# Shifted copies of VectorE's exponentials, divided between VectorE and GpSimd in pieces of 512 columns, with a fifth copy buffer in memory that is dead at the time

## The chip, the cores and the metric

The kernel runs on one core of a Trainium2 chip. The metric is the device time of one execution in microseconds (us). Three runs of the kernel before took 821.25, 820.0 and 817.97 us; their median, 820.0 us, is what the change is held against. Engines are named as in the profile: PE (TensorE, matmuls), ACT (ScalarE), DVE (VectorE), POOL (GpSimd), SP (SyncE, which here only issues DMAs).

## What is computed

One transformer block with modulated layer norms: attention with 32 heads of 16 columns over 2048 tokens of width 512, then a gated feed-forward part with 1792 hidden columns. All tensors are bf16.

```python
def _A_ref(x, wqkv, wo):
    ...
    q, k, v = (qkv[0], qkv[1], qkv[2])
    scores = jnp.einsum('bhqd,bhkd->bhqk', q, k) * Dh ** (-0.5)
    p = _softmax(scores, axis=-1)
    o = jnp.einsum('bhqk,bhkd->bhqd', p, v)
    return (lambda x, *d: x.transpose(*d))(o, 0, 2, 1, 3).reshape(B, S, D) @ wo

def _B_ref(x, w_gate, w_up, w_down):
    return _gelu(x @ w_gate) * (x @ w_up) @ w_down
x = A_x
mod = (_silu(c) @ w_mod).reshape(c.shape[0], 6, 1, -1)
...
h = _layernorm(x, axis=-1) * (1 + ca) + sa
x = x + ga * _A_ref(h, A_wqkv, A_wo)
h = _layernorm(x, axis=-1) * (1 + cb) + sb
x = x + gb * _B_ref(h, B_w_gate, B_w_up, B_w_down)
```

The exponentials of the softmax are the bulk of the elementwise work: 32 x 2048 x 2048 of them, which the kernel handles as 2048 blocks of 128 keys by 512 query columns (or the same amount in narrower pieces).

## The kernel before

**Units, rounds, blocks.** Attention is cut into units (a set of queries, and a quarter of the heads of one parity, `qd` 0 to 7). `SETS` (L32) has nine query sets, seven of 256 queries and two of 128; the first two sets are also handled together at 512 columns for `qd` 0 to 3. A unit runs through the 16 key blocks in rounds; a round is four blocks of 512 columns, one for each of four heads. A round of a 256-column unit covers two key blocks, so such a unit has 8 rounds.

**A tick.** PE writes two or three blocks of scores into one half of six PSUM banks (`ps_sc`). ACT takes them in one instruction, `self.act(self.E..., ACT.Exp)` (L1620), into the ring `E`. The other half of the banks is filled meanwhile.

**VectorE's exponentials.** In many ticks one of the three blocks is not given to ACT. DVE turns it into an approximate exponential by writing `score * 128/OCT + SHIFT_C` as a 16-bit integer (L1628) that is then read as bf16: the integer's upper bits are the exponent, and the lower ones stand in for the mantissa. To make this more exact the kernel takes four versions: the integers as they are, and with 32, 64 and 96 added (`SHIFT`, L72). The added amounts are undone in copies of V (`vs`) that are scaled by the inverse power of two, and PE sums all four. A round handled in this way is called a quad here: four blocks are written to one of the buffers `kq` (four 128x512 instructions out of PSUM), and then three shifted copies of the whole 128x2048 buffer are made into buffers `sq` (three instructions within SBUF). `shift_task` (L1719) queues these copies, one task each. PE then has four sums over V for the round in place of one.

**Which rounds may become quads.** Only those of the last key blocks: `vs` holds copies for the key blocks from `T0` = 12 on (L45, L489). So a 256-column unit can give 2 of its 8 rounds; the first units can give more (`FIRST`, L57; `cand`, L1445). A candidate is dropped when its unit comes near its end (L1581). A quad is begun (L1589) when a `kq` buffer is free, no copy is overdue, DVE's list is short enough (`backlog`, L1283) and the side work isn't too far behind (`credit`).

**Who sets the order.** The kernel is written out by a planner at build time. `_Recorder.rec` (L183) takes each instruction, finds what it must wait for, and keeps a model of when each engine is free (`cost`, L301; `model`, L261). `stream` (L1380) asks this model at each step what could start now: the next tick, the sums over V (`pv_next`), side work (projections, output projection, feed-forward) or a task. `background` (L1291) and `step` (L1255) hand waiting tasks to SP and DVE, by `urgency` (L1243), whenever the model has the engine free. Each engine then executes its own list in that order, and waits for semaphores where it must. So the planner's times decide the order, and the chip's own times decide what that order costs.

**Buffers.** `sq` has four copy buffers (`NSQ`, L48), three of them in `mreg` and one of its own, and two more that serve in parts of the run: `ereg` (also the place of two pieces of the down weights) and half of `onorm`. `room` (L1449) says which may be used when. From when the modulation columns are there (`modB`), a unit has four; the first four units have `ereg` as a fifth.

**Weights.** For the first six sets the feed-forward weights are streamed anew for each set (`load` and `load_down`, L1128 to L1139); from set 6 on they are resident (`weight_parts`, L927), in tensors that attention has finished with. Piece 6 of the gate weights and of the down weights lie in `hreg`, behind `prodL`.

GpSimd does a few memsets and masks at the start, and nothing later.

## Time and profile before

| what | us |
|---|---|
| runs of the kernel before: lowest, median, highest | 817.97, 820.0, 821.25 |
| span of the profiled execution | 817.5 |
| ACT busy | 783.2 |
| PE busy | 750.5 |
| DVE busy | 742.8 |
| POOL busy | 4.6 |

The span runs from the first to the last instruction of the profiled execution; what lies around it (2.5 us to the median) isn't broken down by the profile, and the profiled execution's own time is given by its span alone. In a group of instructions, "mean ns of one" is the time from an instruction's start to its end. On DVE and ACT the next instruction starts before that end, so what an instruction costs its engine is read from the distance of two starts in the timeline, which is shorter. A timeline row gives start, length, engine, line, operation and operands; a row of groups gives count, busy time and mean, then the idle time in front and who ended it.

### The profile page before, as it was taken

The page shows a single profiled execution, that of the slowest core. Times are in us where ns is not written, and L with a number is a line of the kernel's source. Part 1 is how long each engine was busy: PE and PEld are TensorE (multiplying, and loading weights), DVE is VectorE, ACT ScalarE, POOL GpSimd, SP SyncE. Part 2 cuts the span into 40 slices and gives each one's busy share as a digit, 9 for nine tenths or more (in the row PEclk, how much of TensorE's full clock was granted, in tenths as well). Part 3 has the DMA queues.
Part 4 walks back from the last instruction along what each step waited for, and adds up shares of the span by engine and source line. Part 5 has one row for each costly group of instructions (what it writes and reads, how often), then busy time and mean ns, then how long its engine had stood idle before and what let it go on. Part 6 is the DMA issues. An engine that isn't in the chain of part 4 may idle for free.

```text
span 817.5 us, 37365 instructions
## 1 busy us (share of the span) xinstructions
PE 750.5 (92%) x17184; PEld 366.4 (45%) x17188; DVE 742.8 (91%) x1496; ACT 783.2 (96%) x746; POOL 4.6 (1%) x13
## 2 busy tenths in 40 slices
PE   7899999998999898989999899998998899888998
PEld 3333334343543454435443444444443444346567
DVE  6876898899999999999999999999999999989874
ACT  5999999999999999999999999999999999999962
POOL 2000000000000000000000000000000000000000
PEclk9999999999999999999999999999999999999999
DMA  9100000021530153104420442034233541200000
GB/s 292 63 6 20 10 9 10 10 71 40 168 112 16 52 155 93 35 21 134 122 63 16 136 121 61 16 105 133 63 106 88 165 126 36 67 10 10 19 13 14
DMA packets 94499, 57.38 MB, mean 70 GB/s; under 512 B 17029, under 2 KB 91910, under 8 KB 94342
## 3 DMA queue, kind: packets, MB, share of 16 engines
q1 hardware_dynamic: 93812, 54.47, 23.6%
q8 instruction: 134, 2.20, 1.2%
q10 hardware_dynamic: 530, 0.53, 0.2%
q14 instruction: 23, 0.19, 0.1%
HBM read 50.04 MB, written 2.35 MB: 64 GB/s over the span
## 4 chain that ended last, share of the span: by engine, by line
ACT 88%; PE 9%; DVE 1%; issue 0%; DMA 0%; SPq 0%; DVEq 0%
ACT E L341 85%; PE ps_sc L328 4%; PE ps_mi L328 3%; ACT wreg L341 3%; PE ps_pv L328 2%; DMA xs<-in_A_x_dram 0%; DVE osb L362 0%; DVE xs L345 0%; DVE dreg L353 0%; DVE st L381 0%; DVE wreg L353 0%; DVE nwt L345 0%; PE ps_sc L332 0%; DVE wreg L358 0%; DVE mreg L353 0%
## 5 line engine op out<-in xcount | busy, mean ns | idle before, releaser
L341 ACT ACTIVATE E<-ps_sc 128x1024 bf16<-128x1024 f32 (+2 forms) x700 | 758.7, 1319 | 19.1 <-PE ps_sc L328 19.0
L328 PE MATMUL ps_sc<-qT,kT 32*128 32x256 bf16 (+3 forms) x2048 | 202.2, 273 | 25.2 <-ACT E L341 21.1
L328 PE MATMUL ps_sc<-qo,kT 32*128 32x256 bf16 (+2 forms) x2048 | 202.2, 273 | 16.9 <-ACT E L341 15.5
L328 PE MATMUL ps_pv<-E,vaug 128*17 128x256 bf16 (+2 forms) x3204 | 154.1, 273 | 3.8 <-DVE osb L362 2.7
L353 DVE TENSOR_SCALAR dreg<-ps_sc 128x512 uint16<-128x512 f32 x200 | 135.5, 687 | 6.8 <-PE ps_sc L328 5.8
L328 PE MATMUL ps_mi<-wreg,mreg 128*32 128x256 bf16 x2816 | 116.6, 275 | 6.5 <-DVE wreg L362 3.4
L328 PEld LDWEIGHTS ps_sc<-qT,kT 32*128 32x128 bf16 (+1 forms) x2048 | 62.3, 92 | 117.3 <-ACT E L341 105.1
L328 PEld LDWEIGHTS ps_sc<-qo,kT 32*128 32x128 bf16 x2048 | 62.1, 92 | 105.6 <-ACT E L341 94.9
L328 PEld LDWEIGHTS ps_pv<-E,vaug 128*17 128x17 bf16 x3204 | 60.4, 89 | 59.6 <-issue 39.8
L328 PEld LDWEIGHTS ps_mi<-wreg,mreg 128*32 128x32 bf16 x2816 | 63.7, 96 | 42.8 <-issue 24.8
L328 PE MATMUL ps_pv<-mreg,vs 128*17 128x256 bf16 (+2 forms) x1840 | 80.9, 268 | 0.6 <-DVE mreg L353 0.3
L353 DVE TENSOR_SCALAR kq<-ps_sc 128x512 uint16<-128x512 f32 x104 | 70.9, 688 | 8.6 <-PE ps_sc L328 8.2
L353 DVE TENSOR_SCALAR mreg<-dreg 128x2048 uint16<-128x2048 uint16 x100 | 67.5, 682 | 2.2 <-PE ps_pv L328 2.2
L353 DVE TENSOR_SCALAR mreg<-ps_sc 128x512 uint16<-128x512 f32 x96 | 65.0, 688 | 4.5 <-PE ps_sc L328 4.3
L328 PEld LDWEIGHTS ps_pv<-mreg,vs 128*17 128x17 bf16 x1840 | 40.7, 91 | 15.1 <-issue 4.7
L353 DVE TENSOR_SCALAR mreg<-mreg 128x2048 uint16<-128x2048 uint16 x71 | 47.4, 686 | 0.0
L328 PE MATMUL ps_mi<-hreg,wreg 128*32 128x512 bf16 (+1 forms) x496 | 36.6, 376 | 0.4 <-DVE vaug L362 0.3
L362 DVE CAST wreg<-ps_mi 128x512 bf16<-128x512 f32 x49 | 33.6, 686 | 2.4 <-PE ps_mi L328 2.2
L345 DVE TENSOR_TENSOR wreg<-wreg 128x1024 bf16<-128x1024 bf16 (+1 forms) x56 | 34.5, 618 | 0.0
L353 DVE TENSOR_SCALAR sq<-dreg 128x2048 uint16<-128x2048 uint16 x49 | 33.7, 687 | 0.8 <-PE ps_pv L328 0.8
L358 DVE SCALAR_TENSOR_TENSOR wreg<-wreg,ps_mi 128x512 bf16<-128x512 bf16 x49 | 33.4, 682 | 1.0 <-ACT wreg L341 0.5
L353 DVE TENSOR_SCALAR mreg<-kq 128x2048 uint16<-128x2048 uint16 x48 | 32.5, 683 | 0.0
(193 smaller groups left out, 722.7 us busy)
## 6 DMA issues: line engine op xcount, KB each, us to landing
mreg<-in_B_w_up_dram SPq DMA_DIRECT2D x46, 256.0 KB, 3.2
mreg<-in_B_w_gate_dram SPq DMA_DIRECT2D x42, 256.0 KB, 3.3
dreg<-in_B_w_down_dram SPq DMA_DIRECT2D x18, 256.0 KB, 3.5
rb<-scr_rec SPq DMA_DIRECT2D x120, 32.0 KB, 2.0
mreg<-in_B_w_down_dram SPq DMA_DIRECT2D x12, 256.0 KB, 3.7
ereg<-in_B_w_down_dram SPq DMA_DIRECT2D x12, 256.0 KB, 3.8
mreg<-in_w_mod_dram SPq DMA_DIRECT2D x1, 2048.0 KB, 11.8
out_dram<-xs SPq DMA_DIRECT2D x15, 128.0 KB, 1.7
```

What stands on the lines that cost most here:

```text
L328: return self.rec("pe", lambda e: e.matmul(out, lhsT, rhs, start=start, stop=stop, tile_position=tp), [lhsT, rhs], [out], cost=(n, int(rhs ...
L341: return self.rec("act", lambda e: e.activation(out, in_, func, scale=scale, **kw), rd, wr, cost=self.cost("act", out, [in_], "act"))
L345: return self.rec(eng, lambda e: e.tensor_tensor(out, a, b, op), [a, b], [out], cost=self.cost(eng, out, [a, b], "tt"))
L353: return self.rec(eng, lambda e: e.tensor_scalar(out, a, s1, s2, **kw), rd, [out], cost=self.cost(eng, out, [a], "ts") + 60 * (len(rd) - 1 ...
L358: return self.rec("dve", lambda e: e.scalar_tensor_tensor(out, a, s, b, op0=op0, op1=op1), rd, [out], cost=self.cost("dve", out, [a, b], " ...
L362: return self.rec(eng, lambda e: e.tensor_copy(out, in_), [in_], [out], cost=self.cost(eng, out, [in_], "ts"))
```

## The change

Lines of the diff that only pass arguments on are left out.

```diff
+POOL = (0.834, 162)
+PIECE = 512
...
+    def shared(self, eng, out, ins):
+
+        sb = [a for a in ins if self.kind.get(a.tensor.name) == "sb"]
+        return eng == "pool" or len(sb) > 1 or (len(sb) == len(ins) == 1 and self.kind.get(out.tensor.name) == "sb")
...
-        at = 0.0
+        at = self.port_free if port and (eng == "pool" or self.probing is None) else 0.0
...
         self.model(op, max(at, self.free[eng]), cost)
+        if port:
+            self.port_free = op.t1 - 92
...
         if eng == "pool":
-            return n * 3.0 + 100
+            return n * POOL[0] + POOL[1]
...
-        self.sq += [ereg[:, :], onorm[:, 2048:4096]]
+        self.sq += [ereg[:, :], onorm[:, 2048:4096], hreg[:, NFC * 256:NFC * 256 + 2048], mreg[:, 10240:12288]]
...
-        return ([piece(0, i, g[i]) for i in range(6)] + [piece(0, 6, g[6], [("ffn", 0)]), piece(2, 6, d[6], [("ffn", 0)])]
+        return ([piece(0, i, g[i]) for i in range(6)] + [piece(0, 6, g[6], [last, "sq"]), piece(2, 6, d[6], [last, "sq"])]
...
-                self.task([("sp", lambda: self.dma("sp", self.wdst[i], v[:, 2 * i:2 * i + 2, :], "sd%d" % i))], ("wl", gi, 2, i))
+                self.task([("sp", lambda: self.dma("sp", self.wdst[i], v[:, 2 * i:2 * i + 2, :], "sd%d" % i))], ("wl", gi, 2, i),
+                          (lambda: NSQ in self.sq_free) if i > 4 else None)
...
-            e, f = tk[0][0]
+            e, f = tk[0][0][:2]
+            if e == "any":
+                if eng == "pool":
+                    e, f = tk[0][0][2][0]
+                else:
+                    e = "dve"
...
             f()
-            tk[0].pop(0)
+            x = tk[0].pop(0)
+            if x[0] == "any" and eng == "pool":
+                tk[0][0:0] = x[2][1:]
...
         while self.free["dve"] <= t + 150 and self.step("dve", max(self.free["dve"], t) + 40):
             pass
+        while self.free["pool"] <= t + 150 and self.step("pool", max(self.free["pool"], t) + 40):
+            pass
+        while self.free["act"] <= t - 300 and self.step("act", t):
+            pass
...
+            elif pool is self.quad_free:
+                ok = range(NK)
             else:
-                ok = range(NK if pool is self.quad_free else NSQ + (u in units[:4]))
+                ok = list(range(NSQ))
+                if ("ffn", FLOW - 1) in self.have:
+                    ok += [NSQ, NSQ + 3]
+                elif ("q", 3, NDC - 1) in self.have:
+                    ok += [NSQ + 2]
+                elif ("t2T", 0) not in self.have:
+                    ok += [NSQ]
...
+            if ("ffn", FLOW - 1) in self.have and NSQ + 2 in self.sq_free:
+                self.done("sq")
...
-                    elif (... and (pos < ends[FLOW - 1] or self.credit < self.tune[1] or ...
+                    elif (... and (pos < ends[0] or self.credit < self.tune[1] or ...
...
-        def f():
+        def whole():
             s = self.room(self.sq_free, q["rnd"][0])[0]
             self.ts("dve", self.sq[s].bitcast(U16), self.kq[q["k"]].bitcast(U16), float(SHIFT[i]), None, ALU.add)
...
+        def piece(a):
+            s = q["slots"][i + 1] if a else self.room(self.sq_free, q["rnd"][0])[0]
+            c = slice(a, a + PIECE)
+            self.ts("pool", self.sq[s][:, c].bitcast(U16), self.kq[q["k"]][:, c].bitcast(U16), 1.0, float(SHIFT[i]), ALU.mult, ALU.add)
...
+        self.task([("any", whole, [("pool", lambda a=a: piece(a)) for a in range(0, 2048, PIECE)])], ("shift", q["rnd"][0]),
+                  lambda: i + 1 in q["slots"] or bool(self.room(self.sq_free, q["rnd"][0])))
```

A copy is now a task for either engine. If DVE takes it, it is the one 128x2048 instruction of before; if GpSimd takes it, it is four instructions of 128x512 (multiply by 1.0, then add). DVE is offered tasks first, while the planner has it free within 150 ns; then GpSimd. The planner also keeps a time `port_free`: instructions of GpSimd, and those of DVE that read two tensors in SBUF or go from SBUF to SBUF, are placed one after the other, as if they shared one resource. `ereg` is now open to any unit until set 0's feed-forward part begins and again when set 5's is done; in between, a part of `hreg` serves as the fifth copy buffer, and after set 5's feed-forward part a part of `mreg` as a sixth. The last pieces of the gate and down weights, which go to that part of `hreg`, are loaded after set 5's feed-forward part and when the buffer is free, where before they followed set 0's. Two conditions of the planner change as shown: a copy that is open to either engine isn't counted in `backlog`, and from the end of set 0 on (before: set 5) a quad is begun only if the side work isn't too far behind.

More of the change, by code (lines that the diff above doesn't have):

```diff
@@ L345, in tt @@
         return self.rec(eng, lambda e: e.tensor_tensor(out, a, b, op), [a, b], [out],
-                        cost=self.cost(eng, out, [a, b], "tt"))
+                        cost=self.cost(eng, out, [a, b], "tt"), port=self.shared(eng, out, [a, b]))
     def ts(self, eng, out, a, s1, s2, op0, op1=None):
@@ L353, in ts @@
         return self.rec(eng, lambda e: e.tensor_scalar(out, a, s1, s2, **kw), rd, [out],
-                        cost=self.cost(eng, out, [a], "ts") + 60 * (len(rd) - 1 if a.tensor.name not in ("ps_mi", "ps_sc") else len(rd) > 1))
+                        cost=self.cost(eng, out, [a], "ts") + 60 * (len(rd) - 1 if a.tensor.name not in ("ps_mi", "ps_sc") else len(rd) > 1),
+                        port=self.shared(eng, out, [a]))
     def stt(self, out, a, s, b, op0, op1):
@@ L361, in copy @@
     def copy(self, eng, out, in_):
[L362 removed]
+        return self.rec(eng, lambda e: e.tensor_copy(out, in_), [in_], [out], cost=self.cost(eng, out, [in_], "ts"),
+                        port=self.shared(eng, out, [in_]))
     def recip(self, out, in_):
@@ L1440, in stream @@
         self.quad_free = list(range(NK + 1))
-        self.sq_free = list(range(NSQ + 2))
+        self.sq_free = list(range(len(self.sq)))
         self.holds = {}
@@ L1657, in stream @@
                 n = w[4][0]
-                side = (ts <= t + 30 and (self.credit >= n / 2 or "last" in self.have or (self.short(t) > 0 and self.credit > -2048))
+                side = (ts <= t + 30 and (self.credit >= n / 2 or (tq is None and not tp) or "last" in self.have or (self.short(t) > 0 and self.credit > -2048))
                         and n / 2.4 <= gap + max(0, self.free["act"] - self.tune[0] - t - max(0, gap)))
@@ L1812, in tail @@
             t = self.pe_now()
-            while any(self.step(x, max(self.free[x], t) + 40) for x in ("act", "dve", "sp")):
+            while any(self.step(x, max(self.free[x], t) + 40) for x in ("act", "pool", "dve", "sp")):
                 pass
```

20 lines of the change are left out of this document (13 added, 7 removed).

## Prediction

> **What bounds the kernel now.** I read the busy times first, then the chain of waits that ended last, then the busy times by stretch.
>
> ```profile
> span 817.5 us, 37365 instructions
> ...
> PE 750.5 (92%) x17184; PEld 366.4 (45%) x17188; DVE 742.8 (91%) x1496; ACT 783.2 (96%) x746; POOL 4.6 (1%) x13
> ```
>
> ```profile
> ACT 88%; PE 9%; DVE 1%; issue 0%; DMA 0%; SPq 0%; DVEq 0%
> ```
>
> Three engines are over 90% busy, but the chain lies on ACT for 88% of its length. The windows (columns: stretch, its length, then busy us and count of PE, PEld, DVE, ACT and POOL) say where:
>
> ```profile
> core 0: us, PE busy (x) PEld busy (x) DVE busy (x) ACT busy (x) POOL busy (x), PEclk, DMA share, GB/s
> 200.00:700.00 500.00, 464.17 (x10794) 223.77 (x10791) 484.19 (x913) 500.00 (x476) 0.00 (x0) 1.00 0.32 89
> 700.00:750.00 50.00, 43.85 (x1171) 24.33 (x1171) 44.49 (x90) 49.28 (x45) 0.00 (x0) 1.00 0.12 32
> ```
>
> From 200 to 700 us ACT is never idle, so this stretch is as long as ACT's work in it. DVE is busy for 484.19 of the 500 us (96.8%): it can't take much more as it stands. POOL does nothing. The stretch gets shorter only if blocks of exponentials leave ACT, and they can go only to DVE, which needs room for them. PE's figure I don't take for a bound, since it waits for ACT:
>
> ```profile
> PEld ps_sc L328 <- ACT E L341: 135.4, 416, 1.4
> ```
>
> In the same stretch PE's weight loads for the scores wait for ACT 416 times, 135.4 us, 0.33 us on average.
>
> **What a block is worth on ACT.** The groups of ACT in the same stretch:
>
> ```profile
> L341 ACT ACTIVATE E<-ps_sc 128x1024 bf16<-128x1024 f32 x295 | 295.8, 1182 | 0.0
> L341 ACT ACTIVATE E<-ps_sc 128x1536 bf16<-128x1536 f32 x157 | 234.7, 1604 | 0.0
> ```
>
> A third block makes an instruction 1604 - 1182 = 422 ns longer. The number of ticks stays, so a block that moves to DVE saves 0.42 us, and a quad (four blocks) 1.69 us. The stretch has 295 x 2 + 157 x 3 = 1061 blocks on ACT and, below, 295 on DVE: 1356, of which DVE has 21.8%. By the code a 256-column unit may give 2 of 8 rounds, 25%, which is 339 blocks. So there is room for 44 more blocks, 11 quads, and no more.
>
> **What a quad costs DVE.** Two views of DVE's instructions in the same stretch, by line (count, then the shortest, median and longest in ns): the scalar operations of line 353, among them the exponentials out of PSUM and the copies, and the larger two-tensor operations of line 345:
>
> ```profile
> L353 DVE TENSOR_SCALAR dreg<-ps_sc x146: 634/686/693, 211.4 to 698.8; 128x512 uint16<-128x512 f32 x146
> L353 DVE TENSOR_SCALAR kq<-ps_sc x76: 674/687/695, 204.1 to 696.9; 128x512 uint16<-128x512 f32 x76
> L353 DVE TENSOR_SCALAR mreg<-ps_sc x73: 673/687/693, 200.4 to 690.4; 128x512 uint16<-128x512 f32 x73
> L353 DVE TENSOR_SCALAR mreg<-dreg x72: 627/686/695, 221.3 to 692.1; 128x2048 uint16<-128x2048 uint16 x72
> L353 DVE TENSOR_SCALAR mreg<-mreg x57: 630/689/698, 201.9 to 695.7; 128x2048 uint16<-128x2048 uint16 x57
> L353 DVE TENSOR_SCALAR mreg<-kq x36: 629/686/696, 218.0 to 681.5; 128x2048 uint16<-128x2048 uint16 x36
> L353 DVE TENSOR_SCALAR sq<-dreg x36: 631/687/695, 222.5 to 692.7; 128x2048 uint16<-128x2048 uint16 x36
> L353 DVE TENSOR_SCALAR wreg<-wreg x24: 282/419/426, 203.7 to 666.4; 128x1024 bf16<-128x1024 bf16 x18, 128x512 bf16<-128x512 bf16 x6
> L353 DVE TENSOR_SCALAR wreg<-ps_mi,modB x20: 401/405/411, 278.4 to 629.1; 128x256 bf16<-128x256 bf16 x20
> L353 DVE TENSOR_SCALAR sq<-kq x19: 682/686/696, 212.4 to 698.2; 128x2048 uint16<-128x2048 uint16 x19
> ```
>
> ```profile
> L345 DVE TENSOR_TENSOR wreg<-wreg x48: 415/682/694, 202.5 to 667.8; 128x1024 bf16<-128x1024 bf16 x36, 128x512 bf16<-128x512 bf16 x12
> L345 DVE TENSOR_TENSOR hreg<-wreg x24: 389/682/694, 216.1 to 677.6; 128x1024 bf16<-128x1024 bf16 x18, 128x512 bf16<-128x512 bf16 x6
> L345 DVE TENSOR_TENSOR onorm<-osb,rb x21: 680/683/696, 209.0 to 689.8; 128x512 bf16<-128x512 f32 x21
> L345 DVE TENSOR_TENSOR wreg<-ps_mi,gb x12: 680/683/692, 252.9 to 699.4; 128x512 bf16<-128x512 f32 x12
> L345 DVE TENSOR_TENSOR xs<-xs,wreg x11: 424/426/426, 253.6 to 688.8; 128x512 bf16<-128x512 bf16 x11
> ```
>
> 295 exponentials (146 + 76 + 73) and 220 copies (72 + 57 + 36 + 36 + 19). The median of 0.69 us isn't the cost; starts in the timeline (start, length) are:
>
> ```profile
> 506.01 0.69 DVE L353 TENSOR_SCALAR dreg<-ps_sc 128x512 uint16<-128x512 f32 x1
> 506.62 0.68 DVE L353 TENSOR_SCALAR mreg<-mreg 128x2048 uint16<-128x2048 uint16 x1
> 507.22 0.69 DVE L353 TENSOR_SCALAR sq<-kq 128x2048 uint16<-128x2048 uint16 x1
> 507.82 0.69 DVE L353 TENSOR_SCALAR dreg<-ps_sc 128x512 uint16<-128x512 f32 x1
> 508.42 0.68 DVE L345 TENSOR_TENSOR wreg<-ps_mi,gb 128x512 bf16<-128x512 f32 x1
> ```
>
> From the copy at 507.22 to the next instruction are 0.60 us, and from the exponential at 506.01 to the next 0.61. So a quad costs DVE 4 x 0.6 + 3 x 0.6 = 4.2 us now, and 2.4 us if GpSimd makes all copies.
>
> **What a copy costs GpSimd.** The trace of before has no such instruction. The nearest rows:
>
> ```profile
> L369 POOL MEMSET vaug<- 128x512 bf16 x1 | 2.3, 2272 | 0.0
> L369 POOL MEMSET rb<- 128x1024 f32 x1 | 1.2, 1249 | 0.0
> L372 POOL TENSOR_SCALAR_AFFINE_SELECT den<-den 128x4 f32<-128x4 f32 x2 | 0.4, 188 | 0.1
> L372 POOL TENSOR_SCALAR_AFFINE_SELECT self<-self 128x128 f32<-128x128 f32 x1 | 0.3, 308 | 54.8 <-DVE self L369 54.8
> ```
>
> From the two masks, which read and write SBUF (188 ns at 4 columns, 308 at 128), a line through both gives 0.97 ns for a column and 0.68 us for 512. Half of the plain memset of 1024 columns is 0.62 us. The strided memset of 512 columns took 2.27 us, which is the far end; the copies aren't strided, and the row with 1024 plain columns is the nearest in kind. The planner's own price in the diff is 0.834 x 512 + 162 = 589 ns. I take 0.6 us for a piece and 2.4 us for a copy, with 0.59 and 0.68 as the near ends. At 2.27 us a copy would take 9 us, and each would be 6.7 us behind the plan; that end lies above the range and has part of the 2 in 10 that the range leaves out.
>
> **What the sharing costs DVE.** DVE is freed of 0.6 us for each copy that moves. The diff's planner treats GpSimd's pieces and the SBUF instructions of DVE as exclusive. No row here shows a collision, since POOL is idle after its masks, so the wait of a DVE instruction that finds a piece running has these bounds: 0 if both simply run, 0.3 us (half a piece) if it waits for the end, up to 0.9 us if GpSimd's next piece gets in first. I take 0.3, the mean of what the planner assumes. Exponentials come out of PSUM and, in the diff, aren't under this rule.
>
> How many copies move? Under the planner's rule are the 220 copies, the 24 and 48 + 24 + 21 + 11 instructions of `wreg<-wreg`, `hreg<-wreg`, `onorm<-osb,rb` and `xs<-xs,wreg`: 348, about 195 us (0.60 us for those of 0.69; 0.34 for those of 0.42). If the two engines shared every moment, 195 - 0.6 m + 2.4 m = 500, m = 169. The other end is 0. DVE is asked first and GpSimd gets what DVE hasn't reached, so I take the middle, 85.
>
> Then DVE is freed of 85 x 0.6 = 51 us. GpSimd runs 85 x 2.4 = 204 us, 41% of the stretch. Of the 263 DVE instructions left under the rule 41%, or 108, meet a piece and wait 0.3 us: 32 us. The net is 19 us. An added quad costs 2.4 us and the share of its copies that DVE keeps, 3 x 0.6 x 0.6 = 1.1, so 3.5 us. With DVE filled to the same 96.8%: 484.2 - 19 + 3.5 q = 0.968 x (500 - 1.69 q), so q = 3.7 quads, and ACT's stretch is 6.2 us shorter. From 700 to 750 us both engines are nearly as full (ACT 49.28, DVE 44.49 of 50); at the same rate that is 0.6 us. Before 200 us the copy buffers are as before but for `ereg`, and after 750 us there are hardly copies: 0, give or take a quad, 1.7 us. Sum: 6.8 us off the span of 817.5 us, 810.7; the median of the runs lies 2.5 us above that span, so 813.
>
> The Trainium skill, "SBUF — State Buffer", section "Who interferes with whom", says that a GpSimd instruction and a DVE instruction in a two-port mode, or with two SBUF inputs, hold one port pair in turn for their whole length. By that rule the sum is the one above; without it (wait 0) it is the 802 us of the first rival's second case. No run here shows which.
>
> **The parts that I cost at nothing.** Multiply by 1.0 and add is one instruction. The late weight pieces:
>
> ```profile
> L391 SPq DMA_DIRECT2D hreg<-in_B_w_gate_dram x1: 513/513/513, 611.7 to 611.7; - x1
> L391 SPq DMA_DIRECT2D hreg<-in_B_w_down_dram x1: 473/473/473, 619.8 to 619.8; - x1
> ```
>
> ```profile
> DMA to landing us min/median/max: 2.7/3.7/4.7
> ```
>
> They were issued at 611.7 and 619.8 us and land within 4.7. They now follow set 5's feed-forward part, whose last use of streamed down weights, with the first use of the resident ones, is here (first and last start):
>
> ```profile
> L328 PE MATMUL ps_mi<-ereg,hreg x48: 379/389/390, 602.5 to 698.4; 128*32 128x512 bf16 x48
> ...
> L328 PE MATMUL ps_mi<-wreg,hreg x32: 272/273/283, 747.8 to 749.2; 128*32 128x256 bf16 x32
> ```
>
> That leaves 747.8 - 698.4 = 49 us for two loads; if the cover were gone it would be their 2.7 and 4.7 us. On SP they stand ahead of the transfers of the softmax denominators, and could hold those only if PE hadn't finished with the buffer, which the `"sq"` flag has planned as done. The wait of two `ereg` loads for a copy buffer concerns the start of the streamed weights alone. Of the two changed conditions one begins quads more readily (copies aren't counted in the backlog), the other less (credit now counts from set 0 on): a quad either way, 1.7 us.
>
> **New waits.** A DVE instruction that waits for a piece holds the exponentials behind it, these hold their `ps_sc` bank, PE's next scores wait for the bank, and ACT for PE. And PE's sums over a copied buffer wait for the last of four pieces, at least 2.4 us after the first began, against 0.6 us before; all of PE's list stands behind that wait. The planner orders both by its own prices, so they cost only what the chip is slower than those.
>
> **The rivals.**
>
> - *All candidates become quads.* The 11 quads need 56 us of net room on DVE. With waits of 0.3 us that takes about 165 copies on GpSimd, with nearly all of the 500 us of the shared resource in use; with no waits at all 85 copies give 10 quads and 802 us. At 11: 18.6 + 1.9 us less, 797 + 2.5 = 799. For it: POOL has the time. Against it: two engines in turn without a gap.
> - *It moves copies but no time.* If the waits eat what is freed (446 us, which is 484.2 - 51 + 13 for the added quads, and 108 waits of 0.5 us are the 500 us of before), or GpSimd rarely gets a turn: 820. For it: DVE is asked first.
> - *DVE becomes the bound (the slower side).* GpSimd's pieces stand back to back with no wait of their own between them, so the next piece can take its turn before a waiting DVE instruction. From a mean wait of 0.5 us on, DVE's 446 + 108 w is over 500 us. At w = 0.6, a piece for each, it is 511, and the time 817.5 + 11 + 2.5 = 831; at 0.9 it is 543 and 863. For it: the order of pieces is not written out against DVE's by any semaphore. Against it: pieces are short. The Trainium skill, "Perfetto Trace Analysis", section "Optimizing Scalar/DVE Operations", warns that work moved between these two may not help, as they share a port; that speaks for this rival or the one before.
> - *Late copies hold PE.* If a piece takes 0.68 us, a copy is 4 x 0.08 = 0.32 us behind the plan; 85 of them are 27 us on PE. PE's slack of 0.33 us hides part: with half passed on, 820 - 7 + 14 = 827, with all of it 840. The Trainium skill, "GPSIMD Engine Reference", section "Elementwise — side-by-side cycle accounting", gives 769 ns for 512 columns in one kind of loop and about one cycle a column in a lighter one; by the first the copies would be late by 0.7 us each, by the second not.
>
> **How the numbers follow.** Forecast 0.38 (its own range 807 to 816), all candidates 0.12, no time moved 0.12, DVE the bound 0.25, late copies 0.13. About 0.5%, 4 us, is what a measurement of this kernel can tell from no change. Faster: 0.38 + 0.12 = 0.50; same: 0.12; slower: 0.25 + 0.13 = 0.38. The range reaches from just under the first rival to a mean wait of 0.67 us in the third (446 + 72 = 518, 838 us), 798 to 838; left out are part of the first rival and the tails of the last two, under 2 in 10.
>
> **What would show it.** Right: POOL with some 350 to 400 pieces of about 0.6 us; DVE's copies of 128x2048 fewer by about 80 while its 128x512 exponentials rise by about 20; ACT's 128x1536 fewer and 128x1024 more, and ACT still without idle time from 200 to 700 us. DVE's SBUF instructions longer by the wait. Wrong: idle time of ACT behind PE's scores with DVE full (third rival); PE's sums waiting for POOL (fourth); POOL nearly empty, or full with the exponentials unchanged (second); pieces of 1 us and more.

## The result, and the profile after

The changed kernel takes 842.3 us, the median of four runs (840.23 to 847.55), against 819.5 us for the kernel before (817.97 to 821.25, four runs): a ratio of 1.029, with an interval of 1.0269 to 1.0311. It is 22.8 us slower; 813 was forecast, with 798 to 838 as the range.

First the top of the page of the changed kernel, then the shares of the chain of waits that ended last:

```profile
span 840.2 us, 38011 instructions
...
PE 766.0 (91%) x17216; PEld 376.2 (45%) x17216; DVE 720.0 (86%) x1362; ACT 783.9 (93%) x746; POOL 450.1 (54%) x661
...
ACT 42%; PE 28%; DVE 27%; issue 2%; DVEq 0%
```

No engine has become full. ACT's busy time is that of before (783.9 against 783.2), yet its share of the chain fell from 88% to 42%: the rest now passes back and forth between PE and DVE. The windows from 200 to 700 us, with the columns of the prediction:

```profile
200.00:700.00 500.00, 456.92 (x10466) 222.22 (x10454) 450.67 (x781) 484.50 (x456) 303.21 (x436) 0.99 0.31 87
```

ACT was busy for all of the 500 us before; now for 484.50. DVE went from 484.19 to 450.67: it has more room than it had, and still ACT waits. What ACT waits for over the whole execution, with total, times and longest (the row of before ends in 19.0, 18, 5.2):

```profile
ACT E L350 <- PE ps_sc L337: 39.0, 46, 13.1
```

*How lost time on ACT is measured below.* ACT's instructions overlap, so short gaps don't show as idle. I therefore took, for every ACT instruction that starts between 200 and 700 us, the distance to the next start, less 0.8333 ns for each column and 64 ns (82 ns where it reads SBUF). On the kernel before, over 476 instructions, that sum is -0.3 us, so these are ACT's own durations there. On the changed kernel it is 21.7 us. This is the "idle time" of the expectations; the windows show 15.5 us of it.

**Where DVE's time went.** Groups of DVE from 200 to 700 us in the changed kernel (count, busy us, mean ns):

```profile
L362 DVE TENSOR_SCALAR kq<-ps_sc 128x512 uint16<-128x512 f32 x71 | 48.0, 683 | 7.5 <-PE ps_sc L337 6.9
L354 DVE TENSOR_TENSOR wreg<-wreg 128x1024 bf16<-128x1024 bf16 x36 | 30.9, 860 | 0.0
L362 DVE TENSOR_SCALAR mreg<-dreg 128x2048 uint16<-128x2048 uint16 x30 | 25.5, 850 | 3.9 <-PE ps_pv L337 3.9
L354 DVE TENSOR_TENSOR onorm<-osb,rb 128x512 bf16<-128x512 f32 x20 | 16.9, 844 | 0.0
L354 DVE TENSOR_TENSOR hreg<-wreg 128x1024 bf16<-128x1024 bf16 x18 | 16.2, 899 | 0.0
L368 DVE SCALAR_TENSOR_TENSOR rstd<-nwt,rstd 128x2 f32<-128x2 f32 x10 | 2.6, 257 | 0.2
```

Three of these groups before:

```profile
L345 DVE TENSOR_TENSOR wreg<-wreg 128x1024 bf16<-128x1024 bf16 x36 | 24.6, 684 | 0.0
L353 DVE TENSOR_SCALAR mreg<-dreg 128x2048 uint16<-128x2048 uint16 x72 | 48.6, 682 | 0.2 <-PE ps_pv L328 0.2
L358 DVE SCALAR_TENSOR_TENSOR rstd<-nwt,rstd 128x2 f32<-128x2 f32 x10 | 1.6, 158 | 0.2
```

The exponentials out of PSUM are as long as before (683 ns against 688). What goes from SBUF to SBUF is longer by 0.16 to 0.22 us on average: `wreg<-wreg` of 1024 columns 860 ns against 684, `hreg<-wreg` 899 against 682, `onorm<-osb,rb` 844 against 685, the copies `mreg<-dreg` 850 against 682. Instruction by instruction, against the usual length of its group, 126 of them were held, 43.7 us in all, 0.39 us in the middle and none for more than 0.5 us. That is the collision at the shared resource.

GpSimd's pieces, one group of the many, and one in which nothing collides:

```profile
L362 POOL TENSOR_SCALAR mreg<-dreg 128x512 uint16<-128x512 uint16 x212 | 144.9, 709 | 76.4 <-PE ps_pv L337 44.8 <-DVE dreg L362 18.3 <-PE ps_sc L337 12.4
L362 POOL TENSOR_SCALAR ereg<-onorm 128x512 uint16<-128x512 uint16 x4 | 2.4, 615 | 0.0
```

A piece alone takes 0.62 us, and 0.71 us with its own waits. There are 648 pieces, so 162 copies.

**How a wait on DVE reaches ACT.** The timeline of the changed kernel (start, length, engine, operation, then in brackets the idle time in front and who ended it):

```profile
223.54 3.67 POOL L362 TENSOR_SCALAR mreg<-kq 128x512 uint16<-128x512 uint16 x4 [1.16 <-PE ps_pv L337]
223.62 1.09 DVE L362 TENSOR_SCALAR sq<-mreg 128x2048 uint16<-128x2048 uint16 x1
224.76 0.40 PE L337 MATMUL ps_pv<-sq,vs 128*17 128x256 bf16 x8 [0.62 <-DVE sq L362]
225.64 1.09 DVE L354 TENSOR_TENSOR hreg<-wreg 128x1024 bf16<-128x1024 bf16 x1
226.65 1.10 DVE L362 TENSOR_SCALAR mreg<-kq 128x2048 uint16<-128x2048 uint16 x1
227.68 0.67 DVE L372 CAST wreg<-ps_mi 128x512 bf16<-128x512 f32 x1
228.40 0.84 PE L337 MATMUL ps_mi<-wreg,mreg 128*32 128x256 bf16 x24 [1.17 <-DVE wreg L372]
230.04 1.02 ACT L350 ACTIVATE E<-ps_sc 128x1024 bf16<-128x1024 f32 x1 [0.80 <-PE ps_sc L337]
232.86 1.02 ACT L350 ACTIVATE E<-ps_sc 128x1024 bf16<-128x1024 f32 x1 [1.80 <-PE ps_sc L337]
```

Read it from the top. At 223.54 GpSimd starts a piece; the DVE copy issued at 223.62 takes 1.09 us in place of 0.68. PE's sums over that copy stand idle for 0.62 us. The next SBUF instructions of DVE are 1.09 and 1.10 us long too, so the conversion `wreg<-ps_mi`, itself undisturbed, starts late at 227.68; PE's list has feed-forward matmuls that need it in front of the next scores, and waits 1.17 us. The scores come late, and ACT stands still for 0.80 us. Nothing here is full: it is three lists, each worked off in order, behind one another. Added up from 200 to 700 us, PE stands idle behind DVE for 19.5 us (42 times), against 6.9 (16 times) before.

The 1.80 us at the end have a further cause, which the windows around 230.5 us show (the column behind POOL is the granted TensorE clock):

```profile
226.50:230.40 3.90, 2.33 (x60) 1.37 (x52) 3.90 (x6) 3.10 (x4) 3.62 (x5) 1.00 0.36 96
230.50:233.90 3.40, 3.30 (x52) 1.46 (x52) 2.87 (x6) 1.59 (x2) 2.98 (x5) 0.50 0.70 205
```

For 3.4 us the clock is half, so the scores that come late also take longer. There is a second such stretch at 373.8 us, and none between 200 and 700 us before. In both, PE had been busy for only about 60% of the 3.4 to 3.9 us ahead. Of ACT's 21.7 us, 4.2 are lost inside these two stretches or within 3 us behind them. Whether PE's pauses bring the lower clock on was not tested.

**The end.** In both kernels ACT loads a table after the last exponentials and then waits for the last tiles. The timelines, before and after:

```profile
788.53 0.60 PE L328 MATMUL ps_mi<-xs,hreg 128*32 128x512 bf16 x8
789.52 1.28 ACT L341 ACT_TABLE_LOAD   x1
```

```profile
804.34 1.28 ACT L350 ACT_TABLE_LOAD   x1
807.99 2.76 PE L337 MATMUL ps_mi<-xs,hreg 128*128 128x512 bf16 x12
811.97 2.76 PE L337 MATMUL ps_mi<-xs,hreg 128*128 128x512 bf16 x12 [0.78 <-DVE xs L354]
818.93 0.60 ACT L350 ACTIVATE E<-ps_sc 128x512 bf16<-128x512 f32 x1 [13.10 <-PE ps_sc L337]
```

Before, set 6's down projection for the same two tiles was done between the scores, by 789.1. After, both tiles' sums run behind the last exponentials, and the last tile's first gelu, ACT's next work but for an instruction of one column, starts 14.6 us after the table load; before it was 6.7 us (789.5 to 796.2). So of the 22.7 us between the two spans 14.8 arise before the table load and 7.9 behind it.

### The profile page after: what moved, and what is told of

Same layout as the page of the kernel before. It is cut to its first block, busy times and chain, and to the rows that moved or that the text cites. A ratio compares the mean times of both kernels' runs of the same rounds, so it can differ in the third digit from the quotient of the medians.

```text
span 840.2 us, 38011 instructions
## 1 busy us (share of the span) xinstructions
PE 766.0 (91%) x17216; PEld 376.2 (45%) x17216; DVE 720.0 (86%) x1362; ACT 783.9 (93%) x746; POOL 450.1 (54%) x661
## 4 chain that ended last, share of the span: by engine, by line
ACT 42%; PE 28%; DVE 27%; issue 2%; DVEq 0%
ACT E L350 41%; PE ps_mi L337 11%; PE ps_sc L337 10%; PE ps_pv L337 7%; DVE dreg L362 5%; DVE mreg L362 5%; DVE wreg L354 2%; DVE kq L362 2%; DVE wreg L368 2%; DVE sq L362 1%; DVE onorm L354 1%; ACT wreg L350 1%; DVE hreg L354 1%; DVE xs L354 1%; DVE wreg L372 1%
## 5 line engine op out<-in xcount | busy, mean ns | idle before, releaser
L337 PE MATMUL ps_sc<-qT,kT 32*128 32x256 bf16 (+3 forms) x2048 | 206.9, 273 | 16.6 <-ACT E L350 12.2
L337 PE MATMUL ps_sc<-qo,kT 32*128 32x256 bf16 (+2 forms) x2048 | 203.7, 274 | 17.6 <-ACT E L350 14.8
L362 POOL TENSOR_SCALAR mreg<-dreg 128x512 uint16<-128x512 uint16 x212 | 144.9, 709 | 76.4 <-PE ps_pv L337 44.8
L362 POOL TENSOR_SCALAR mreg<-mreg 128x512 uint16<-128x512 uint16 x96 | 65.3, 703 | 38.7 <-PE ps_pv L337 19.1
L362 POOL TENSOR_SCALAR sq<-dreg 128x512 uint16<-128x512 uint16 x76 | 53.6, 725 | 46.6 <-PE ps_pv L337 28.5
L362 POOL TENSOR_SCALAR sq<-kq 128x512 uint16<-128x512 uint16 x40 | 27.4, 700 | 88.0 <-DVE kq L362 87.3
L362 POOL TENSOR_SCALAR mreg<-kq 128x512 uint16<-128x512 uint16 x76 | 52.1, 706 | 41.6 <-DVE kq L362 18.8
L337 PE MATMUL ps_pv<-mreg,vs 128*17 128x256 bf16 (+2 forms) x1552 | 69.2, 269 | 1.6 <-issue 0.9
L354 DVE TENSOR_TENSOR wreg<-wreg 128x1024 bf16<-128x1024 bf16 (+1 forms) x56 | 43.7, 780 | 0.0
L362 POOL TENSOR_SCALAR hreg<-kq 128x512 uint16<-128x512 uint16 x36 | 27.4, 783 | 26.0 <-PE ps_sc L337 12.4
L337 PEld LDWEIGHTS ps_pv<-mreg,vs 128*17 128x17 bf16 x1552 | 34.9, 91 | 12.5 <-issue 5.5
```

What stands on the lines that cost most here:

```text
L337: return self.rec("pe", lambda e: e.matmul(out, lhsT, rhs, start=start, stop=stop, tile_position=tp), [lhsT, rhs], [out], cost=(n, int(rhs ...
L354: return self.rec(eng, lambda e: e.tensor_tensor(out, a, b, op), [a, b], [out], cost=self.cost(eng, out, [a, b], "tt"), port=self.shared(e ...
L362: return self.rec(eng, lambda e: e.tensor_scalar(out, a, s1, s2, **kw), rd, [out], cost=self.cost(eng, out, [a], "ts") + 60 * (len(rd) - 1 ...
```

## The experiments

Two theories stood at the start. *Collisions*: DVE's waits at the shared resource pass through PE's list to ACT. *Order*: the new conditions and buffers lead the build to a worse order, whatever GpSimd does. The prediction's fourth rival, late copies, was tested with them. "Lost" is ACT's lost time from 200 to 700 us as defined above, "end" the time from the table load to the first gelu.

| run | us, median | ratio to before (interval) | lost | end |
|---|---|---|---|---|
| before | 819.5 | 1 | -0.3 | 6.7 |
| changed | 842.3 | 1.029 (1.0269 to 1.0311) | 21.7 | 14.6 |
| e1 pieces of 8 columns | 826.1 | 1.008 (1.0058 to 1.0106) | 2.2 | 14.1 |
| e2 without GpSimd | 832.4 | 1.015 (1.0124 to 1.0172) | 8.2 | 12.5 |
| e3 sharing alone | 835.5 | 1.018 (1.0144 to 1.0216) | 15.2 | 13.1 |
| e4 later sums | 840.8 | 1.026 (1.0234 to 1.0277) | 18.3 | 8.3 |
| e5 turns enforced | 863.1 | 1.054 (1.0511 to 1.056) | 34.8 | 14.0 |
| e6 half pieces | 830.2 | 1.012 (1.0084 to 1.0158) | 3.0 | 14.3 |
| e7 two half pieces | 850.8 | 1.038 (1.0355 to 1.0401) | 21.7 | 14.6 |
| e8 other order | 834.7 | 1.019 (1.0165 to 1.0212) | 24.5 | 6.7 |
| e9 other order, two halves | 847.7 | 1.035 (1.0315 to 1.0374) | 24.5 | 6.4 |
| e10 before, other order | 820.0 | 0.999 (0.9974 to 1.0012) | 0.9 | 9.2 |
| e11 e2, copies counted | 820.5 | 1.001 (0.9996 to 1.0029) | 0.7 | 5.4 |
| e12 e8, pieces of 8 columns | 813.8 | 0.994 (0.9911 to 0.9962) | 2.0 | 6.7 |
| e13 changed, copies counted | 844.3 | 1.031 (1.0282 to 1.0338) | 22.7 | 10.3 |
| e14 fifth buffer alone | 817.4 | 0.999 (0.9969 to 1.0011) | 7.1 | 4.8 |

**e1 and e6: the same order, shorter pieces.** Every engine's list is that of the changed kernel. GpSimd computes only the first 8, or 256, of the 512 columns of each piece; the copy buffers are set to 1 once at the start where nothing else has written them. These twelve memsets have a price of their own in some executions: in the profiles of e6 and e12 (below) a DVE instruction of the first layer norm is held behind them for 4.2 us, and the eleventh of ACT's exponentials starts some 5 us later than in the kernel with the same order (31.0 us against 25.7, and 29.6 against 25.2); in that of e1 it isn't held. The times of e6 and e12 are thus rather too long.

```diff
-            self.ts("pool", self.sq[s][:, c].bitcast(U16), self.kq[q["k"]][:, c].bitcast(U16), 1.0, float(SHIFT[i]), ALU.mult, ALU.add)
+            out, in_ = self.sq[s][:, c].bitcast(U16), self.kq[q["k"]][:, c].bitcast(U16)
+            self.rec("pool", lambda e: e.tensor_scalar(out[:, 0:8], in_[:, 0:8], 1.0, float(SHIFT[i]), ALU.mult, ALU.add), [in_], [out],
+                     cost=self.cost("pool", out, [in_], "ts"), port=True)
```

> Each GpSimd piece computes only the first 8 of its 512 columns (the rest of each copy keeps what lay in the buffer; three buffers are filled once near the start); PE, ACT, DVE and SP keep exactly the order of the changed kernel, and the planner prices the pieces as before. Collision theory (VectorE's SBUF instructions wait while a piece runs, PE's list waits for VectorE, ACT for PE): pieces of about 0.2 us leave next to no waits, DVE's SBUF instructions are back at 0.68 us, ACT's idle time from 200 to 700 us (15.5 us in the changed kernel) falls under 3 us, and the time falls by 18 to 24 us, to 818 to 824. Plan theory (the new order itself is worse, whatever GpSimd does): the time stays at 838 to 843 and ACT's idle time stays.

> The changed kernel with every engine's order kept; each piece of GpSimd computes 256 of its 512 columns (the other columns of the copy keep the value 1, so the weights of those heads are left out), about half as long as 0.617 us. If the cost is VectorE's waits for the piece under way (linear in the length of a piece): between 826.1 (8 columns) and 842.3 (512 columns), near 834 us, with ScalarE's idle time at 200 to 700 us near 11 us and a median wait of VectorE near 0.2 us. If waits under some size are taken up by the buffers between the engines, so that only the longest are passed on: 826 to 830. If the number of pieces counts and not their length: 838 to 842.

The windows of e1, then of e6, from 200 to 700 us:

```profile
200.00:700.00 500.00, 466.87 (x10884) 228.47 (x10886) 432.92 (x812) 498.20 (x476) 102.25 (x452) 1.00 0.31 88
```

```profile
200.00:700.00 500.00, 465.76 (x10841) 227.18 (x10839) 438.28 (x816) 497.33 (x474) 210.00 (x447) 1.00 0.32 88
```

With 8 columns DVE's waits are gone (2 instructions, 0.13 us) and 16.2 us of the loss with them; ACT is busy for 498.20 us again. So the collisions cost 16 us in this order, whatever part the halved clock has in it: in this stretch the profile of e1 has no halved clock, where the changed kernel lost 4.2 us. The other 6 us stay, and they stand at the end: 14.1 us behind the table load, while the exponentials end at 786.2, 3.3 us earlier than before. Half pieces still hold 50 instructions of DVE for 9.3 us, 0.20 in the middle and none over 0.3. If each wait were passed on, ACT would lose 2.2 + (9.3 / 43.7) x 19.5 = 6.4 us, or 5.5 without the 4.2 us at the halved clock; it loses 3.0. Short waits are partly taken up; PE's weight loads for scores had 0.33 us in hand on average in the kernel before, which fits.

**e2 and e3: the change without GpSimd, and the sharing alone.** In e2 GpSimd is never offered a copy, the rest of the change stays. In e3 the buffers, the order of the weight pieces, the condition on beginning quads and the ACT step in `background` are those of before. So is a third condition that the change altered and the extract under "The change" doesn't show: side work may now start, whatever the credit, when neither a tick nor sums stand ready. The copies stay uncounted in `backlog` in both runs.

```diff
-        while self.free["pool"] <= t + 150 and self.step("pool", max(self.free["pool"], t) + 40):
-            pass
...
-        if not self.step("sp", None) and not self.step("pool", None) and not self.step("dve", None):
+        if not self.step("sp", None) and not self.step("dve", None):
...
```

> The changed kernel with GpSimd never offered a copy: VectorE makes all of them, the other parts of the change (buffers, weight order, conditions of the planner) stay. Collision theory: ACT is without idle time in the stretch from 200 to 700 us, and the time is 815 to 825. Plan theory (buffers, late weights or the new conditions cost the time): 832 or more, with the set 6 feed-forward part still unfinished when the last exponential is done.

> The sharing alone: buffers, weight order and the conditions for side work and for beginning quads as in the kernel before. Collision theory: as slow as the changed kernel, 832 to 845, with 10 us or more of idle time of ACT between 200 and 700 us. Plan theory: 822 or less.

Each half alone is slower than before, by 12 and 15 us; the sum is more than the 22.8 of both. The two aren't a clean division, since the uncounted copies are in each. That e2 loses at all was a surprise, since its 260 exponentials of 1536 columns and 432 of 1024 are those of before. It is taken up in e11.

**e4: sums ready later in the build's reckoning.** The build takes the sums over a copied buffer as ready 600 ns later when it chooses what PE does next.

```diff
-SAFE = 0
+SAFE = 600
```

> The changed kernel with 600 ns added to the time at which the planner takes a quad's sums to be ready (SAFE = 600), so PE takes them up later. Late-copy theory (PE is held by copies that come later than planned): ACT's idle time between 200 and 700 us falls by more than half, and the time by 10 us or more, to 832 or less. Collision theory, with PE held through VectorE's other results (casts, products, normalised tiles): less than 6 us, 836 to 846.

840.8 us: hardly a change, though the order is another one (the end is 6.3 us shorter, the table load comes 5.4 us later). In the changed kernel PE waits for POOL only 0.4 us in all. Late copies, the fourth rival, play no part.

**e5: the planned turns enforced.** Each instruction under the rule of `shared` waits for the other engine's last such instruction ahead of it in the build's order.

```diff
+        if port:
+            for s, n in self.last_port.items():
+                if s != eng and needs.get(s, 0) < n:
+                    needs[s] = n
+            self.last_port[eng] = seq
         self.count[stream] = seq
```

> The changed kernel with its order on every engine kept, and one wait added to each instruction that uses the port shared by VectorE and GpSimd: it waits by a semaphore for the other engine's last such instruction that stands ahead of it in the build's order. So the turns at the port are the planned ones. Theory A (VectorE loses its turns to pieces that come at other moments than planned, and that is why the plan's cover does not hold): the 43.7 us of VectorE's waits at 200 to 700 us fall, ScalarE's idle time there from 21.7 us to under 8, and the time comes to 826 to 833 us. Theory B (the waits are those of the plan, or the delay of a turn costs the same wherever it falls): no better than 840; with a semaphore's delay at each change of turns, 842 to 855.

Windows and chain of e5:

```profile
200.00:700.00 500.00, 451.10 (x10168) 216.81 (x10168) 405.73 (x760) 475.60 (x442) 249.74 (x418) 0.99 0.30 84
```

```profile
POOL 32%; PE 27%; DVE 26%; ACT 11%; issue 4%; DVEq 0%; POOLq 0%
```

The instructions no longer collide (one of DVE's is held for 0.4 us), yet it is the slowest run, 863.1 us: the wait has only moved in front of the instruction, and POOL now has a third of the chain. So enforcing the planned turns doesn't win the loss back. How much of the 21 us over the changed kernel is the semaphores' own delay stays open, and with it whether the planned turns would help at no delay.

**e7: nothing left out, two half pieces in place of one.**

```diff
+            def parts(e):
+                for x in range(0, PIECE, PART):
+                    r = e.tensor_scalar(out[:, x:x + PART], in_[:, x:x + PART], 1.0, float(SHIFT[i]), ALU.mult, ALU.add)
+                return r
+            self.rec("pool", parts, [in_], [out], cost=self.cost("pool", out, [in_], "ts"), port=True)
```

> The changed kernel with every engine's order kept; each piece of 512 columns is computed by two instructions of 256 columns, one behind the other, so that nothing is left out. GpSimd's work grows (by the half pieces of e6, about 0.42 us each where nothing holds them, a copy takes 3.3 us where it took 2.4). If what counts is how long VectorE waits for the one instruction under way: near e6, 829 to 834 us, with waits under 0.3 us. If VectorE's waits add up over both halves, or the longer copies hold TensorE's sums: 838 to 846.

PE's waits for POOL in e7, and its windows:

```profile
PE ps_pv L338 <- POOL mreg L1773: 5.5, 12, 0.9
PE ps_pv L338 <- POOL sq L1773: 1.6, 3, 1.1
PE ps_pv L338 <- POOL hreg L1773: 1.4, 3, 0.5
```

```profile
200.00:700.00 500.00, 458.20 (x10424) 220.95 (x10416) 439.58 (x789) 482.53 (x454) 390.87 (x864) 0.99 0.31 85
```

850.8 us: worse. DVE's waits fall only to 29.5 us (139 of them). One of them alone is 4.7 us:

```profile
586.43 2.25 POOL L1773 TENSOR_SCALAR mreg<-dreg 128x256 uint16<-128x256 uint16 x6
586.78 5.38 DVE L355 TENSOR_TENSOR onorm<-osb,rb 128x512 bf16<-128x512 f32 x1
588.64 2.98 POOL L1773 TENSOR_SCALAR sq<-dreg 128x256 uint16<-128x256 uint16 x8
593.46 1.45 ACT L351 ACTIVATE E<-ps_sc 128x1536 bf16<-128x1536 f32 x1 [3.80 <-PE ps_sc L338]
```

Thirteen half pieces start while this DVE instruction, 0.68 us long by itself, stands, and it ends 0.54 us behind the last of them; ACT then waits 3.80 us. Earlier in e7 a copy is held for 3.4 us in the same way (at 107.3 us), and in e9 two instructions for 2.7 and 4.2 us (at 141.6 and 179.4). Besides, GpSimd's copies, which take it 391 us now in place of 303, come late for PE's sums, 8.7 us. Part of the time is a lower clock: its mean over an execution is 0.982 to 0.990 here, against 0.986 to 0.998 in the changed kernel, and at like clocks the difference is about 4 us (851.87 at 0.984 against 847.55 at 0.986). How the 21.7 us that ACT loses are shared among these isn't told apart.

**e8, e9 and e12: another order of the same work.** Three of the four weights by which the build opens quads and offers tasks are altered (the expectation says two); e9 adds the two halves of e7, e12 the 8 columns of e1.

```diff
-TUNE = ((600, 3500, 6, 120),) * 16
+TUNE = ((600, 4000, 4, 60),) * 16
```

> The changed kernel built with two of the build's four weights of its order altered (TUNE 600, 4000, 4, 60 for 600, 3500, 6, 120), which gives another order of the same work: 107 quads in all for 105, and by the build's own reckoning little of set 6's feed-forward network left behind the last exponentials. If the 7.9 us behind the last exponentials come from where the order leaves that network's sums: the stretch from the last exponentials to the last tile's first gelu falls from 14.6 us to about 7, and the time to 831 to 836 us; the collisions stay (ScalarE's idle time at 200 to 700 us near 20 us). If the stretch is long for another reason (the collisions themselves delay the sums): over 838.

> Both at once: the order of the run before this one, with each piece computed by two instructions of 256 columns. If the two costs (waits at the port, the end of the order) are separate, the gains add: 842.3 less about 11 less about 8, so 820 to 827 us. If both remove the same idle time: 829 to 834.

> The order of e8 (834.7 us), each piece computing 8 of its 512 columns as in e1 (most of the weights of those heads are left out), with every engine's order kept. If the collisions alone keep that order above before: 834.7 less 16 to 20, so 815 to 819 us, below before, with ScalarE's idle time at 200 to 700 us from 24.5 us to under 4; what the sharing is worth at no price at the port is then 1 to 5 us, near the 6.8 us of the sum. If ScalarE's idle time comes from the order itself: over 825.

The windows of e8, then of e12, then the chain of e12:

```profile
200.00:700.00 500.00, 459.48 (x10561) 225.23 (x10558) 464.28 (x800) 482.41 (x459) 321.91 (x461) 0.99 0.31 87
```

```profile
200.00:700.00 500.00, 469.00 (x10986) 231.92 (x10978) 442.47 (x830) 498.05 (x480) 109.66 (x484) 1.00 0.32 89
...
ACT 85%; PE 11%; DVE 3%; issue 1%; DMA 0%; SPq 0%; DVEq 0%
```

In e8 the end is 6.7 us as before, and the time falls by 7.6 us to 834.7; what ACT loses between 200 and 700 us stays, 24.5 us. e12 then takes the collisions away, and the time falls by another 20.9 us to 813.8, 5.3 us under the kernel before (rather more without the delay by the memsets). The two parts of the loss are separate, and the collisions alone turn a small gain into a loss. e9 was expected at 820 to 827 and came to 847.7: the two halves cost 12.9 us in this order, 8.5 in that of e7, clock included (at a mean clock of 0.988 e8 took 837.27 us and e9 846.49).

**e10 and e11: what a new order costs without collisions.** e10 is the kernel before with other weights of the order, chosen because the build reckons its end near that of before. e11 is e2 with the copies counted in DVE's backlog again; in the change they carry the mark `any`, and the count passes over them.

```diff
-            if steps[0][0] == "dve" and (when is None or when()):
-                n += next((i for i, s in enumerate(steps) if s[0] != "dve"), len(steps))
+            if steps[0][0] in ("dve", "any") and (when is None or when()):
+                n += next((i for i, s in enumerate(steps) if s[0] not in ("dve", "any")), len(steps))
```

> The kernel before, without anything of the change, built with three of the four weights altered (TUNE 600, 5000, 8, 30), so in another order of the same work. If a new order by itself costs nothing: 815 to 823 us. If the order of before is a well hit one, and a redrawn order costs some us whatever redraws it (which would explain the 5.6 us of e1 and part of the 12 of e2): 824 to 835.

> The kernel of e2 (the change without GpSimd) with one thing altered: the count of VectorE's backlog, which must be under 6 for a quad to open, counts the copies again. In the change they carry the mark any in place of dve, and the count passes over them, so quads open while copies still stand in VectorE's list. If that mark is what cost the 12 us of e2: 815 to 823 us, with ScalarE's idle time at 200 to 700 us from 8.2 us to under 2. If the buffers, the late weight pieces or the changed conditions cost it: 828 to 834 as in e2.

The windows of e2, then of e11:

```profile
200.00:700.00 500.00, 461.60 (x10641) 223.16 (x10638) 471.61 (x890) 492.35 (x466) 0.00 (x0) 1.00 0.31 88
```

```profile
200.00:700.00 500.00, 462.51 (x10736) 221.17 (x10734) 480.46 (x903) 499.18 (x474) 0.00 (x0) 1.00 0.31 88
```

e10 is as fast as before, so a new order need not cost anything; it is one order, and a chosen one. e11 is as fast, too (820.5 us), so the 12 us of e2 are the uncounted copies: quads open while copies still stand in DVE's list, and from 200 to 700 us ACT is idle for 7.7 us in e2 and for 0.8 in e11, and the end is 12.5 against 5.4. The fifth buffer, the late weight pieces and the other conditions cost nothing there.

**e13 and e14.** e13 is the changed kernel, with GpSimd, with the same count; e14 has no GpSimd, the count, the fifth buffer, the gate of before and other weights of the order (600, 7000, 6, 75).

> The changed kernel, with GpSimd, and the copies counted in VectorE's backlog again. If the mark costs here what it cost without GpSimd, 842.3 less about 6 to 12: 830 to 836 us. If the collisions hold the end whatever the count does: 838 to 844.

> No GpSimd, the copies counted, the fifth buffer and the weights' order as in the change, the old gate, and two of the four weights of the order altered (TUNE 600, 7000, 6, 75). If a fifth buffer and a fitting order are worth something on the chip: 814 to 818 us, under before. If not: 819 to 823.

e13 gains nothing, 844.3 us: the end is 4.3 us shorter, but with collisions ACT's lost time stays (22.7 us) and the exponentials end later. e14 is at 0.999 of before, between 0.9969 and 1.0011, so no better that can be told; of the 7.1 us lost in its profile 4.5 lie in or just behind three stretches of halved clock. None of the kernels that leave nothing out beats the kernel before.

## Why the prediction was wrong

*What held.* ACT was the bound, and from 200 to 700 us. The pieces: 0.6 us forecast, 0.62 measured. The collisions: 108 instructions of DVE with 0.3 us each, 32 us, were forecast; 126 with 0.35 us, 43.7 us, were measured. Copies that move in that stretch: 85 forecast, about 110 measured (436 pieces). Quads: 3.7 and a rest forecast; ACT's exponentials of 1536 columns went from 260 to 244, 16 blocks, which is 4 quads and 6.8 us of ACT. That count agrees partly by luck: the sum took it from a DVE filled to 96.8%, but DVE has room left (90%), and the number is what the build's own reckoning gives (6 with the weights of e8). The rule of the Trainium skill, "SBUF — State Buffer", section "Who interferes with whom", is borne out: instructions from SBUF to SBUF and those with two SBUF inputs wait, in the changed kernel by no more than one piece (0.5 us at most), exponentials out of PSUM (683 ns) don't.

*The step that failed* is in "New waits": that a DVE instruction that waits holds PE and then ACT was named there, and then costed at nothing, because "the planner orders both by its own prices, so they cost only what the chip is slower than those". The sum charged DVE's 32 us of waits to DVE's room alone. The runs show them a second time, on ACT: 43.7 us of waits on DVE became 21.7 us lost on ACT from 200 to 700 us (4.2 of them at and behind the halved clock) with DVE only 90% busy, and e1 and e12, which remove the waits and keep the order, win back 16.2 and 20.9 us. That is two to three times the 6.8 us of the gain. The Trainium skill, "Perfetto Trace Analysis", section "Optimizing Scalar/DVE Operations", says that work moved between these two might not help, since they share a port; here, in the order of e8, it would be worth 5.3 us and the port takes 20.9.

*A second, smaller one*: "the parts that I cost at nothing" put the changed conditions at a quad either way, 1.7 us, and didn't name the third, on side work (it costs nothing in e11, which has it). Without GpSimd the uncounted copies cost 12 us (e2 against e11). In the changed kernel the order leaves set 6's down projection behind the last exponentials, 7.9 us; e8, with other weights, ends as before. Which edit puts it there isn't settled. The uncounted copies have a part: counting them shortens the end in both pairs, by 7.1 us without GpSimd (e2, e11) and by 4.3 with it (changed, e13). But e8 leaves them uncounted and has 6.7 us, and e10, with nothing of the change, has 9.2.

*The rivals.* The third had the right sign and the right engine, but another mechanism: in the changed kernel pieces don't get in one after another (no wait over 0.5 us), and DVE isn't full; with pieces of half the size they do (e7 and e9, waits of 2.7 to 4.7 us), so the mechanism exists. Its point, a mean wait of 0.5 us, was set by DVE's throughput; what decides is whether the wait fits into what PE has in hand. The first two fall with the 4 quads, the fourth with e4.

*Its working with the right price* would have been 817.5 - 6.8 + 21.7 + 7.9 = 840.3 for the span, against 840.2; the two added terms are measured ones and could not be had from the trace of before, but one bound could: all 32 us passed on through PE and ACT, 817.5 - 6.8 + 32 + 2.5 = 845, belonged among the rivals.

## What to carry to other kernels

A wait put on an engine that isn't the bound is not paid out of that engine's idle time when the engines work through lists in order: ask what the bounding engine has in hand against that delay (here about 0.33 us), and price the waits a second time there. Before work is shared with GpSimd, count how many of VectorE's instructions use the shared ports and multiply by half a piece; here 0.4 us of waits (43.7 us for 110 copies) came with every copy that saved VectorE 0.6. And when a task gets a new mark, look for every count that reads the old one: that alone was worth 12 us in the build without GpSimd, and nothing in the build with it (e13).

## What the runs showed of the hardware

The collision holds even tiny instructions: `rstd<-nwt,rstd`, 2 columns of f32 with two inputs in SBUF, takes 257 ns on average, 158 before; the diff's rule doesn't cover this kind. It doesn't lengthen instructions that read PSUM, nor the statistics of the layer norm with one SBUF input (`BATCH_NORM_STATS2`, 678 ns against 680). And cutting an instruction in two doesn't halve what it holds up: two half pieces of 0.48 us on average, waits included, stand for one of 0.71, and DVE's waits fell only from 43.7 to 29.5 us, 4.7 of which are a single wait behind thirteen half pieces in a row.

A DVE instruction that waits doesn't always get in between two GpSimd instructions: the four long waits of e7 and e9 each end 0.54 us behind the last of a row of half pieces, and at the start of e6 and e12 an instruction of four columns is held for 4.2 us by memsets. With pieces of 512 columns no wait was over 0.5 us. What decides between the two isn't known.

The TensorE clock drops to half for 3.4 us at a time, here and there for 6.8 or 10.2, and in the places looked at behind a stretch in which PE had paused: in e7 PE is busy for 1.02 of the 4 us from 588 to 592, and the clock is half from 592.3 on. Among the changed kernel's four executions the one with the lowest mean clock is the longest (847.55 us at 0.986) and the one with the highest the shortest (840.23 at 0.998).
